# Forget logits in packets of 768 bytes, spread by GpSimd, and logit sums behind the scans

## The chip, the cores and the metric

One core of a Trainium2 chip runs the program. The metric is the device time of one execution in microseconds (us). TensorE (PE) does the matmuls and transposes, VectorE (DVE), ScalarE (ACT) and GpSimd (POOL) the element-wise work, and SyncE (SP) issues nearly all DMA transfers, in the order in which they are written.

## The reference

Gated linear attention over 4 batches, 8 heads, 768 tokens and 48 channels a head gives 3072 tokens of 384 channels. They pass a mixture of 8 experts with one expert a token, and then a block with two up-projections that are multiplied with each other and two projections behind them. The change touches the attention alone:

```python
f = 1.0 / (1.0 + np.exp(-f_logit))
for t in range(S):
    state = f[:, :, t, :, None] * state + np.einsum('bhd,bhe->bhde', k[:, :, t], v[:, :, t])
    y[:, :, t] = np.einsum('bhd,bhde->bhe', q[:, :, t], state)
...
logits = xn @ en.T / tau
expert_idx = np.argmax(logits, axis=1)
```

Here `f_logit` is stored as [batch, head, token, channel], so one token of one head is a run of 48 floats, 192 bytes, and neighbouring tokens of one head follow each other.

## The kernel before

The tokens are cut into 24 units of 128 (6 chunks of each of the 4 batches). The attention is a software pipeline that is written out by hand under `tc.manual_schedule()`: a loop of 26 turns (lines 758 to 788) calls a list of small steps, `parts` (lines 749 to 754), each on the unit that its second entry says: `(s_score, 2)` means that turn i works on unit i - 2. Every engine runs its instructions in the order in which the turns emit them, so the order in the list is the order in each queue.

For one unit, f is loaded to `fs` with the 128 tokens on the partitions and 8 heads of 64 columns (48 channels and a filling of ones). `s_pre` (line 398) makes the gate from the logits a turn ahead: ACT takes tanh(f/2), GpSimd scales it by 0.5 and adds 0.5, in place; only unit 0 does both on ACT, in two halves. `s_gate` (407) transposes the gates on PE, two heads at a time, four transposes into one PSUM bank, so that channels lie on the partitions and tokens along the row. `s_scan` (411) runs the two cumulative products on DVE. `s_qk` (427) transposes q and k and multiplies them by the products (`qd`, `kd`, on DVE); `s_score`, `s_mask`, `s_kb`, `s_inter`, `s_out`, `s_uu` do the attention inside the unit and the state. `s_xt` (518) transposes the result back and adds columns for the expert logits; ACT copies the tokens out, and `s_lg` (530) sums the logit columns on DVE, which releases the PSUM bank. Banks come from a pool of 6 in the order of use.

Beside this the pipeline converts weights that come as 64-bit numbers: `cvt.words` (248) on ACT reads a tile `raw`, `cvt.bits` (259) on DVE, `cvt.sums` (265) on GpSimd. The first `raw` tiles are needed in turn 6. `turn` is called four times a turn and takes the next piece of each routing generator `route` (565): ranking of the tokens on DVE and PE, then scatters of the tokens to DRAM, issued by GpSimd (624). `make_en` (538) normalises the expert vectors once, in pieces spread over turns 0 to 3.

At the end of each turn SP issues the loads: f of unit i + 3, k and q of i + 2, v of i (768 to 771), a `raw` tile, and in some turns a filling of the scatter target with zeros (786). `fs`, `ks`, `qs` have 3 buffers each. `load` (375) gives one DMA a unit and tensor: 128 partitions, 8 runs of 192 bytes on each. `warm` (385) issues matmuls on ones that compute nothing needed: 18 at the start, 24 in turn 0, 16 in turn 1.

Behind the attention come the routing's last groups, then the experts (`g1_step`, `g2_step`, with `xs_prep`, whose transposes at line 872 write every fourth word of a PSUM bank) and the last block (`ab_step`, `out_step`).

Of the kernel before, what the change touches and what calls it, by code (L numbers as in the profile page):

```python
# [7 lines left out]
F32 = mybir.dt.float32  # L8
# [3 lines left out]
AF = mybir.ActivationFunctionType  # L12
ALU = mybir.AluOpType
# [6 lines left out]
def attn_moe_glu_kernel(  # L20
# [18 lines left out]
    B, H, S, D = q.shape  # L39
    N, DM = out.shape  # L40
    E, _, FF = w1.shape
    P = 128
# [316 lines left out]
    ks = [ld.tile([P, H, 64], F32, name=f"k{i}") for i in range(NB)]  # L359
    fs = [ld.tile([P, H, 64], F32, name=f"f{i}") for i in range(NB)]  # L360
    NV = 4
# [13 lines left out]
    def load(src, tiles, u):  # L375
        if 0 <= u < NU:
# [4 lines left out]
            )  # L381

    st = {}

# [13 lines left out]
    def s_pre(u):  # L398
        for hs in (slice(H // 2, H), slice(0, H // 2)) if u == 0 else (slice(0, H),):
            f = fs[u % NB][:, hs, 0:D]  # L400
            A.activation(out=f, in_=f, func=AF.Tanh, scale=0.5)
            if u == 0:
                A.activation(out=f, in_=f, func=AF.Identity, scale=0.5, bias=half[:, 0:1])
            else:
                G.tensor_scalar(out=f, in0=f, scalar1=0.5, scalar2=0.5, op0=ALU.mult, op1=ALU.add)

    def s_gate(u):
        js = (range(NP // 2, NP), range(0, NP // 2)) if u == 0 else (range(NP),)
        st["f", u] = [(j[0], j[-1] + 1, tpair(fs[u % NB], "f", "acc", j)) for j in js]

# [127 lines left out]
    def make_en():  # L538
        spare = cv.tile([P, 512, 2], I32, name="raw", bufs=RAW)[0:E].bitcast(F32).rearrange("e n w -> e (n w)")
        raw, et = spare[:, 0:DM], spare[:, 512:512 + DM]  # L540
        ep = cv.tile([P, 512], F32, name="gt", bufs=2)[0:E].rearrange("e (h d) -> e h d", h=H)
        s = rt.tile([E, 6], F32, name="es")
        SP.dma_start(out=raw, in_=emb)
        SP.dma_start(out=s[:, 4:5], in_=tau.to_broadcast([E, 1]))
        yield
        G.memset(ep, 0.0)
        sq = wk.tile([P, DM], F32, name="sq", bufs=1)[0:E]
        A.activation(out=sq, in_=raw, func=AF.Square, accum_out=s[:, 0:1])
        G.tensor_tensor(out=s[:, 1:2], in0=s[:, 0:1], in1=half[0:E, 0:1], op=ALU.pow)
        G.tensor_scalar(out=s[:, 1:2], in0=s[:, 1:2], scalar1=1e-6, scalar2=None, op0=ALU.add)  # L550
        V.tensor_tensor(out=s[:, 2:3], in0=s[:, 1:2], in1=s[:, 4:5], op=ALU.mult)
        V.reciprocal(out=s[:, 3:4], in_=s[:, 2:3])
        yield
        G.tensor_tensor(out=et, in0=raw, in1=s[:, 3:4].to_broadcast([E, DM]), op=ALU.mult)
        G.tensor_tensor(out=ep[:, :, 0:D], in0=raw.rearrange("e (h d) -> e h d", h=H), in1=s[:, 3:4].unsqueeze(2).to_broadcast([E, H, D]), op=ALU.mult)
        yield
        b = bank([P, KD + NP, E], "eb")
        for j in range(KD):
            PE.transpose(out=b[:, j, :], in_=et[:, j * P:(j + 1) * P], identity=ident[0:E, 0:E])
        for j in range(NP):  # L560
            PE.transpose(out=b[:, KD + j, :], in_=ep[:, 2 * j:2 * j + 2, :].rearrange("e h d -> e (h d)"), identity=ident[0:E, 0:E])
        A.copy(out=enT, in_=b[:, 0:KD, :])
        A.copy(out=sel[:, :, 2 * D:], in_=b[:, KD:, :])

    def route(u0, n):
# [26 lines left out]
        V.tensor_reduce(out=nb, in_=O.rearrange("p g e -> p e g"), axis=AX.X, op=ALU.add)  # L592
        V.tensor_scalar(out=r0, in0=r0, scalar1=1e-6, scalar2=None, op0=ALU.add)
        yield
# [5 lines left out]
        for i in range(n - 1):  # L600
# [3 lines left out]
            )  # L604
        V.tensor_tensor(out=d, in0=L, in1=wide(mx), op=ALU.subtract)
        V.reciprocal(out=rinv, in_=r0)
        yield
# [70 lines left out]
    with tc.manual_schedule():  # L678
        for hs0 in (slice(H // 2, H), slice(0, H // 2)):
            SP.dma_start(out=fs[0][:, hs0, 0:D], in_=f_logit[0, hs0, 0:P, :].rearrange("h p d -> p h d"))  # L680
        load(k, ks, 0)
        load(f_logit, fs, 1)
        load(q, qs, 0)
# [3 lines left out]
        load(q, qs, 1)  # L687
        load(f_logit, fs, 2)
        V.memset(ones, 1.0)
        warm(18)  # L690
        V.memset(fs[0][:, :, D:], 1.0)
        G.memset(ident, 0.0)
# [9 lines left out]
        V.memset(half, 0.5)  # L702
        V.memset(half[:, 2:3], 0.0)
        for i in range(1, NB):
            V.memset(fs[i][:, :, D:], 1.0)
            V.memset(qs[i][:, :, D:], 0.0)
            V.memset(ks[i][:, :, D:], 0.0)
# [37 lines left out]
        def turn():  # L745
# [5 lines left out]
            (s_kb, 2), (cvt.lower, 2), (s_pre, -1), (cvt.sums, 1), (s_sm, 1), (s_xt, 4), (cvt.words, 0), (s_blocks, 2),  # L751
            (s_scan, 0), (turn, None), (turn, None), (turn, None), (turn, None), (cvt.bits, 0), (s_inter, 3), (s_lg, 4),
            (s_sq, 4), (s_out, 3), (cvt.upper, 1), (s_uu, 3),
# [4 lines left out]
        for i in range(NU + 2):  # L758
# [7 lines left out]
            if i - 4 in groups:  # L766
                routing.append(route(*groups[i - 4]))
            load(f_logit, fs, i + 3)
            load(k, ks, i + 2)
# [6 lines left out]
            if i in (0, 1):  # L776
                warm((24, 16)[i])
            if i == 0:
# [384 lines left out]
```

## Time and profile before

| | us |
|---|---|
| median of 3 runs | 741.42 (739.48 to 742.17) |
| profiled execution | 740.17 |
| its span, first to last instruction | 738.4 |
| attention stage in it, to the last score matmuls | about 151 |

The profile is of one execution. Times in it count from the span's start. An instruction's line number is that of the kernel before; a helper's line can be shared by several callers, and the tile names tell them apart. A row of a timeline gives start and duration in us, engine, line, operation, output<-inputs, shapes, the count of merged instructions and, in brackets, how long the engine stood idle before and what ended that. Matmuls overlap, so the duration of one is not its share of PE's time; the distance of two starts is.

### The profile page before, as it was taken

The page shows a single profiled execution, that of the slowest core. Times are in us where ns is not written, and L with a number is a line of the kernel's source. Part 1 is how long each engine was busy: PE and PEld are TensorE (multiplying, and loading weights), DVE is VectorE, ACT ScalarE, POOL GpSimd, SP SyncE. Part 2 cuts the span into 40 slices and gives each one's busy share as a digit, 9 for nine tenths or more (in the row PEclk, how much of TensorE's full clock was granted, in tenths as well). Part 3 has the DMA queues.
Part 4 walks back from the last instruction along what each step waited for, and adds up shares of the span by engine and source line. Part 5 has one row for each costly group of instructions (what it writes and reads, how often), then busy time and mean ns, then how long its engine had stood idle before and what let it go on. Part 6 is the DMA issues. An engine that isn't in the chain of part 4 may idle for free.

```text
span 738.4 us, 12730 instructions
## 1 busy us (share of the span) xinstructions
PE 721.0 (98%) x4849; PEld 663.9 (90%) x4849; DVE 347.2 (47%) x673; ACT 338.4 (46%) x703; POOL 338.9 (46%) x422
## 2 busy tenths in 40 slices
PE   7999999999999999999999999999999999999995
PEld 7989989988899998999999988988888888888885
DVE  7889899956564555354353232322322322323222
ACT  4688787864566575475554542112112122121210
POOL 6356696893977686474574862102202202221002
PEclk9999999999999999999999999999999999999999
DMA  8999999826668668745433330000100100100001
GB/s 170 219 199 212 224 242 213 217 94 203 213 198 263 211 209 255 222 145 153 129 124 93 123 87 1 15 29 1 44 1 0 44 1 0 44 1 19 25 1 46
DMA packets 132156, 86.47 MB, mean 117 GB/s; under 512 B 106481, under 2 KB 114681, under 8 KB 132089
## 3 DMA queue, kind: packets, MB, share of 16 engines
q1 hardware_dynamic: 128489, 75.34, 38.3%
q0 software_dynamic: 3072, 9.46, 3.4%
q8 instruction: 40, 0.66, 0.4%
q10 hardware_dynamic: 528, 0.79, 0.3%
q14 instruction: 27, 0.22, 0.1%
HBM read 70.57 MB, written 15.01 MB: 116 GB/s over the span
## 4 chain that ended last, share of the span: by engine, by line
PE 71%; issue 10%; POOL 6%; DMA 5%; DVE 3%; ACT 3%; SPq 1%; POOLq 0%; ACTq 0%; DVEq 0%
PE acc L899 13%; PE hb L885 12%; PE pa L981 10%; PE pb L981 10%; PE ob L994 10%; PE wpb L177 3%; PE a L442 2%; DMA stg<-in_moe_w_dram 2%; PE y L476 2%; POOL xsd L624 2%; PE xl L522 2%; DMA raw<-in_moe_w_out_dram 1%; PE y L468 1%; PE f L393 1%; PE xb L872 1%
## 5 line engine op out<-in xcount | busy, mean ns | idle before, releaser
L135 POOL TENSOR_TENSOR wl<-stg,wh 128x384 fp32r<-128x384 f32 (+1 forms) x121 | 138.6, 1175 | 61.9 <-ACT wh L134 60.0
L984 DVE TENSOR_TENSOR a<-a,pb 128x512 f32<-128x512 f32 x48 | 33.0, 687 | 181.6 <-PE pb L981 175.3
L994 PE MATMUL ob<-wp,ab 128*128 128x384 f32 x576 | 108.2, 339 | 0.0
L994 PEld LDWEIGHTS ob<-wp,ab 128*128 128x128 f32 x576 | 102.3, 188 | 3.8
L899 PE MATMUL acc<-h,wh 128*128 128x448 f32 (+7 forms) x384 | 104.2, 351 | 1.5 <-DVE h L888 1.0
L885 PE MATMUL hb<-xT,wh 128*128 128x448 f32 (+7 forms) x384 | 102.6, 348 | 0.0
L981 PE MATMUL pa<-x,wh 128*128 128x512 f32 x288 | 90.2, 394 | 0.0
L981 PE MATMUL pb<-x,wh 128*128 128x512 f32 x288 | 89.9, 393 | 0.0
L888 DVE SCALAR_TENSOR_TENSOR h<-hb,h 128x448 fp32r<-128x448 f32 (+7 forms) x64 | 37.0, 578 | 105.4 <-ACT h L887 104.9
L983 ACT COPY a<-pa 128x512 f32<-128x512 f32 x48 | 28.1, 586 | 120.6 <-PE pa L981 120.6
L1001 POOL DMA_INDIRECT out_dram<-o,didx x24 | 23.2, 965 | 129.4 <-DVE o L1000 126.0
L135 POOL TENSOR_TENSOR x<-xd,x 128x512 fp32r<-128x512 f32 x18 | 22.8, 1290 | 120.4 <-ACT x L134 120.4
L986 ACT CAST ab<-a 128x512 fp32r<-128x512 f32 x48 | 29.8, 621 | 104.5 <-DVE a L984 104.5
L134 ACT CAST wh<-stg 128x384 fp32r<-128x384 f32 (+1 forms) x124 | 62.7, 563 | 28.8 <-DMA stg<-in_moe_w_dram 22.4
L899 PEld LDWEIGHTS acc<-h,wh 128*128 128x128 f32 x384 | 70.4, 188 | 4.8 <-DVE h L888 2.2
L885 PEld LDWEIGHTS hb<-xT,wh 128*128 128x128 f32 x384 | 70.8, 188 | 1.4
L885 PE MATMUL hb<-xT,wl 128*128 128x448 f32 (+7 forms) x192 | 66.7, 348 | 0.0
L899 PE MATMUL acc<-h,wl 128*128 128x448 f32 (+7 forms) x192 | 66.7, 347 | 0.0
L981 PEld LDWEIGHTS pb<-x,wh 128*128 128x128 f32 x288 | 54.2, 188 | 12.7
L887 ACT ACTIVATE h<-hb 128x448 fp32r<-128x448 f32 (+7 forms) x64 | 32.4, 506 | 68.6 <-PE hb L885 68.4
L981 PEld LDWEIGHTS pa<-x,wh 128*128 128x128 f32 x288 | 53.6, 188 | 9.2
L981 PE MATMUL pb<-x,wl 128*128 128x512 f32 x144 | 56.9, 395 | 0.0
(185 smaller groups left out, 1288.5 us busy)
## 6 DMA issues: line engine op xcount, KB each, us to landing
stg<-in_moe_w_dram SPq DMA_DIRECT2D x31, 768.0 KB, 5.7
raw<-in_moe_w_dram SPq DMA_DIRECT2D x28, 512.0 KB, 5.3
xs<-xsd SPq DMA_DIRECT2D x8, 675.5 KB, 6.0
k<-in_k_dram SPq DMA_DIRECT2D x24, 192.0 KB, 5.2
q<-in_q_dram SPq DMA_DIRECT2D x24, 192.0 KB, 4.9
v<-in_v_dram SPq DMA_DIRECT2D x24, 192.0 KB, 4.5
f<-in_f_logit_dram SPq DMA_DIRECT2D x23, 192.0 KB, 3.9
raw<-in_moe_w_out_dram SPq DMA_DIRECT2D x8, 384.0 KB, 5.2
```

What stands on the lines that cost most here:

```text
L134: A.copy(out=hi, in_=src)
L135: eng.tensor_tensor(out=lo, in0=src, in1=f32(hi), op=ALU.subtract)
L885: PE.matmul(out=b, lhsT=w[x][:, kk, cs], rhs=xT[e][y][:, kk, :], start=(kk + n == 0), stop=(kk == KD - 1 and n == 2))
L887: A.activation(out=h[0], in_=b, func=AF.Relu)
L888: V.scalar_tensor_tensor(out=h[1], in0=b, scalar=0.0, in1=f32(h[0]), op0=ALU.max, op1=ALU.subtract)
L899: PE.matmul(out=acc[d], lhsT=w[x][:, s % 4, d * P:(d + 1) * P], rhs=hs[s][y], start=(s + n == 0), stop=(s == KF - 1 and n == 2))
L981: PE.matmul(out=b, lhsT=w[x][:, kk, cs], rhs=x2[n][y][:, kk, :], start=(kk + m == 0), stop=(kk == KD - 1 and m == 2))
L983: A.copy(out=t, in_=pa)
L984: V.tensor_tensor(out=t, in0=t, in1=pb, op=ALU.mult)
L986: A.copy(out=ab[s][0], in_=t)
L994: PE.matmul(out=oacc[t], lhsT=ab[s][x][:, t * P:(t + 1) * P], rhs=wp[:, y, s, :], start=(s + m == 0), stop=(s == KF - 1 and m == 2))
L1001: ins = G.indirect_dma_start(out=out, out_offset=bass.IndirectOffsetOnAxis(ap=didx[:, j:j + 1], axis=0), in_=o, in_offset=None,)
```

## The change

`load_f` takes the place of `load` for f of units 1 to 23. It issues four DMAs a unit, one for each pair of heads, each to 32 partitions: a partition holds four neighbouring tokens of two heads, so that a run is 4 x 48 floats, 768 bytes. ACT takes the tanh in this layout; GpSimd's scaling writes into a second tile, `gs`, of two buffers, where the heads are spread to 64 columns again; and `s_gate` transposes the four tokens of a partition one after the other and writes each to every fourth column of the bank. Unit 0 keeps its layout, in `gs[0]`. Beside that: `s_lg` moves from behind `s_inter` to directly behind `s_scan`, ahead of the routing pieces and `cvt.bits`; the add of 1e-6 to the norms in `route` moves from ahead of the rank matmuls to behind them; one product in `make_en` moves from DVE to GpSimd and the reciprocal behind it a turn later; and the warm-up matmuls of turn 0 go from 24 to 14.

```diff
-    fs = [ld.tile([P, H, 64], F32, name=f"f{i}") for i in range(NB)]
+    TQ = 4
+    fs = [ld.tile([P, 2, TQ * D], F32, name=f"f{i}") for i in range(NB)]
+    gs = [ld.tile([P, H, 64], F32, name=f"g{i}") for i in range(2)]
...
+    def load_f(u):
+        if 0 <= u < NU:
+            b, c = units[u]
+            for j in range(NP):
+                SP.dma_start(
+                    out=fs[u % NB][j * P // NP:(j + 1) * P // NP],
+                    in_=f_logit[b, 2 * j:2 * j + 2, c * P:(c + 1) * P, :].rearrange("h (p t) d -> p h (t d)", t=TQ),
+                )
...
     def s_pre(u):
-        for hs in (slice(H // 2, H), slice(0, H // 2)) if u == 0 else (slice(0, H),):
-            f = fs[u % NB][:, hs, 0:D]
+        if u:
+            f = fs[u % NB]
             A.activation(out=f, in_=f, func=AF.Tanh, scale=0.5)
-            if u == 0:
+            to = gs[u % 2].rearrange("p (t h) d -> p t h d", h=2)[:, :, :, 0:D]
+            G.tensor_scalar(out=to, in0=f.rearrange("p h (t d) -> p t h d", d=D), scalar1=0.5, scalar2=0.5, op0=ALU.mult, op1=ALU.add)
+        else:
+            for hs in (slice(H // 2, H), slice(0, H // 2)):
+                f = gs[0][:, hs, 0:D]
+                A.activation(out=f, in_=f, func=AF.Tanh, scale=0.5)
                 A.activation(out=f, in_=f, func=AF.Identity, scale=0.5, bias=half[:, 0:1])
-            else:
-                G.tensor_scalar(out=f, in0=f, scalar1=0.5, scalar2=0.5, op0=ALU.mult, op1=ALU.add)
 
     def s_gate(u):
-        js = (range(NP // 2, NP), range(0, NP // 2)) if u == 0 else (range(NP),)
-        st["f", u] = [(j[0], j[-1] + 1, tpair(fs[u % NB], "f", "acc", j)) for j in js]
+        if u == 0:
+            st["f", u] = [(j[0], j[-1] + 1, tpair(gs[0], "f", "acc", j)) for j in (range(NP // 2, NP), range(0, NP // 2))]
+            return
+        t = bank([P, NP, P], "f", "acc")
+        for i in range(TQ):
+            src = gs[u % 2][:, 2 * i:2 * i + 2, :].rearrange("p h d -> p (h d)")
+            PE.transpose(out=t.rearrange("q j (p t) -> q t j p", t=TQ)[:, i], in_=src, identity=ident)
+        st["f", u] = [(0, NP, t)]
...
-        V.tensor_tensor(out=s[:, 2:3], in0=s[:, 1:2], in1=s[:, 4:5], op=ALU.mult)
+        G.tensor_tensor(out=s[:, 2:3], in0=s[:, 1:2], in1=s[:, 4:5], op=ALU.mult)
+        yield
         V.reciprocal(out=s[:, 3:4], in_=s[:, 2:3])
-        yield
...
         V.tensor_reduce(out=nb, in_=O.rearrange("p g e -> p e g"), axis=AX.X, op=ALU.add)
-        V.tensor_scalar(out=r0, in0=r0, scalar1=1e-6, scalar2=None, op0=ALU.add)
         yield
...
         V.tensor_tensor(out=d, in0=L, in1=wide(mx), op=ALU.subtract)
+        V.tensor_scalar(out=r0, in0=r0, scalar1=1e-6, scalar2=None, op0=ALU.add)
         V.reciprocal(out=rinv, in_=r0)
...
-        load(f_logit, fs, 1)
+        load_f(1)
...
-        load(f_logit, fs, 2)
+        load_f(2)
...
-            (s_scan, 0), (turn, None), (turn, None), (turn, None), (turn, None), (cvt.bits, 0), (s_inter, 3), (s_lg, 4),
+            (s_scan, 0), (s_lg, 4), (turn, None), (turn, None), (turn, None), (turn, None), (cvt.bits, 0), (s_inter, 3),
...
-            load(f_logit, fs, i + 3)
+            load_f(i + 3)
...
-                warm((24, 16)[i])
+                warm((14, 16)[i])
```

## Rows read from the trace of the kernel before

**Rows 1.** The page: busy engines over the span; DMA share in 40 slices, in tenths.

```profile
PE 721.0 (98%) x4849; PEld 663.9 (90%) x4849; DVE 347.2 (47%) x673; ACT 338.4 (46%) x703; POOL 338.9 (46%) x422
...
DMA  8999999826668668745433330000100100100001
```

**Rows 2.** Stretches: length, busy us (instructions) of PE, PEld, DVE, ACT, POOL; clock, DMA share, GB/s.

```profile
8.00:19.00 11.00, 9.50 (x104) 8.67 (x104) 9.16 (x17) 4.50 (x11) 6.28 (x11) 1.00 1.00 197
34.00:37.00 3.00, 3.00 (x50) 2.85 (x50) 2.93 (x5) 1.35 (x3) 1.25 (x3) 1.00 1.02 346
190.00:200.00 10.00, 10.00 (x50) 9.16 (x49) 3.31 (x3) 4.79 (x11) 10.00 (x9) 1.00 0.99 336
```

**Rows 3.** Timeline of PE, line 442 alone: the score matmuls that open a turn.

```profile
15.48 1.16 PE L442 MATMUL a<-qd,kd 64*128 64x128 f32 x16 [1.45 <-DVE kd L434]
...
36.48 1.16 PE L442 MATMUL a<-qd,kd 64*128 64x128 f32 x16
43.96 1.16 PE L442 MATMUL a<-qd,kd 64*128 64x128 f32 x16
50.21 1.16 PE L442 MATMUL a<-qd,kd 64*128 64x128 f32 x16
...
62.71 1.16 PE L442 MATMUL a<-qd,kd 64*128 64x128 f32 x16
69.60 1.16 PE L442 MATMUL a<-qd,kd 64*128 64x128 f32 x16
...
107.76 1.16 PE L442 MATMUL a<-qd,kd 64*128 64x128 f32 x16
115.25 1.16 PE L442 MATMUL a<-qd,kd 64*128 64x128 f32 x16
```

**Rows 4.** Timelines of ACT and PE where they stood for a weight tile.

```profile
37.34 0.55 ACT L256 ACTIVATE gt<-raw 128x384 int32<-128x384 uint32 x1 [1.75 <-DMA raw<-in_moe_w_out_dram]
...
62.46 0.57 ACT L256 ACTIVATE gt<-raw 128x384 int32<-128x384 uint32 x1 [1.20 <-DMA raw<-in_moe_w_out_dram]
...
107.41 0.69 ACT L256 ACTIVATE g<-raw 128x512 int32<-128x512 uint32 x1 [1.45 <-DMA raw<-in_moe_w_dram]
...
39.69 0.63 PE L393 MATMUL kt<-ident,k 128*128 128x128 f32 x4 [1.03 <-ACT sq L528]
```

**Rows 5.** Timeline of the first 15 us: warm-up matmuls and DVE's first products.

```profile
5.44 2.77 PE L388 MATMUL warm<-ones 128*128 128x128 bf16 x24
...
9.63 0.69 DVE L433 TENSOR_TENSOR qd<-qt,w 128x512 f32<-128x512 f32 x1 [1.62 <-PE qt L393]
...
9.87 1.06 PE L388 MATMUL warm<-ones 128*128 128x128 bf16 x16
...
13.49 0.56 DVE L551 TENSOR_TENSOR es<-es 8x1 f32<-8x1 f32 x1
```

**Rows 6.** Line 378's issues on SP: ns min/median/max, first and last start.

```profile
L378 SPq DMA_DIRECT2D k<-in_k_dram x24: 395/1236/1922, 1.9 to 133.8; - x24
L378 SPq DMA_DIRECT2D q<-in_q_dram x24: 580/1796/4526, 3.0 to 135.0; - x24
...
L378 SPq DMA_DIRECT2D f<-in_f_logit_dram x23: 368/378/807, 2.4 to 128.1; - x23
```

**Rows 7.** The chain that ended last: start, us, what; transposes with and without strided output.

```profile
45.71 0.44 PE qt L393 x4
...
210.78 1.10 PE xb L872 x12
```

**Rows 8.** Line 405, GpSimd's scaling of the gates: ns min/median/max, first and last start.

```profile
L405 POOL TENSOR_SCALAR f<-f x23: 502/512/517, 6.5 to 137.8; 128x384 f32<-128x384 f32 x23
```

**Rows 9.** Timeline of DVE at 109 us: the logit sum and the bit operations before it.

```profile
109.60 0.68 DVE L262 TENSOR_SCALAR raw<-z 128x512 int32<-128x512 int32 x1
110.31 0.69 DVE L263 SCALAR_TENSOR_TENSOR raw<-z,raw 128x512 int32<-128x512 int32 x1
110.92 0.18 DVE L532 TENSOR_REDUCE lg<-xl 128x8 f32<-128x32 f32 x1
```

**Rows 10.** Timelines of ACT and GpSimd where the chain of scatters begins.

```profile
143.53 0.48 ACT L523 COPY xt<-xl 128x384 f32<-128x384 f32 x1 [1.27 <-PE xl L522]
...
147.53 1.22 POOL L449 TENSOR_SCALAR_AFFINE_SELECT am<-am 128x512 f32<-128x512 f32 x2 [2.02 <-ACT am L448]
```

More of the change, by code (lines that the diff above doesn't have):

```diff
@@ L679, in attn_moe_glu_kernel @@
         for hs0 in (slice(H // 2, H), slice(0, H // 2)):
-            SP.dma_start(out=fs[0][:, hs0, 0:D], in_=f_logit[0, hs0, 0:P, :].rearrange("h p d -> p h d"))
+            SP.dma_start(out=gs[0][:, hs0, 0:D], in_=f_logit[0, hs0, 0:P, :].rearrange("h p d -> p h d"))
         load(k, ks, 0)
-        load(f_logit, fs, 1)
+        load_f(1)
         load(q, qs, 0)
@@ L687, in attn_moe_glu_kernel @@
         load(q, qs, 1)
-        load(f_logit, fs, 2)
+        load_f(2)
         V.memset(ones, 1.0)
         warm(18)
-        V.memset(fs[0][:, :, D:], 1.0)
+        V.memset(gs[0][:, :, D:], 1.0)
         G.memset(ident, 0.0)
@@ L703, in attn_moe_glu_kernel @@
         V.memset(half[:, 2:3], 0.0)
+        V.memset(gs[1][:, :, D:], 1.0)
         for i in range(1, NB):
-            V.memset(fs[i][:, :, D:], 1.0)
             V.memset(qs[i][:, :, D:], 0.0)
```

## The prediction

> **What bounds the kernel now.** I read the page first. TensorE (PE) is busy 98% of the span and the DMA digits stand at 8 to 9 for the first eight slices, some 148 us, and fall after that [rows 1]. So the change, which touches only the attention stage at the head of the program, meets two nearly full resources there: PE and the 16 DMA engines. The table of stretches tells what fills the DMA engines: in 8 to 19 us, with nothing but the 192-byte packets of k, q, v and f on the way, a share of 1.00 moves 197 GB/s; in 34 to 37 us, with the 3072-byte rows of w_out, a share of 1.02 moves 346 GB/s; and in the bulk weight loads of 190 to 200 us, 0.99 moves 336 GB/s [rows 2].
>
> Next the timeline of PE at line 442, the score matmuls, which open every turn of the loop. Two neighbours tell the length of a turn: 43.96 to 50.21 is 6.25 us, and that is the time of the matmuls themselves: neither row shows idle time of PE before it. A longer turn holds a stall: 36.48 to 43.96 is 7.48, a stall of 1.2 us; 62.71 to 69.60 is 6.89, 0.6 us; 107.76 to 115.25 is 7.49, 1.2 us, of which I count 1.1 because that turn also holds the short routing matmuls. The turn before 15.48 shows a PE gap of 1.45 us that ended with DVE's kd [rows 3]. All that this change can take from the stage is in such stalls, about 5 us with the start; the rest of the stage is matmuls that it keeps. Then ACT and PE at those stalls: ACT stood 1.75, 1.20 and 1.45 us for a converted weight tile (raw) that had not landed, and PE's gap of 1.03 us in the first of them ended when ACT got through [rows 4]. So the stalls begin as late transfers and reach PE through ACT. Last the tail: at 143.53 ACT stood 1.27 us for PE, and at 147.53 GpSimd (POOL) stood 2.02 us for ACT [rows 10]. GpSimd's chain of scatters, which sets the end of the stage, therefore starts when PE gets there, and what PE gains before 143 us reaches the end one for one. Behind the stage the weights follow the routing result, so the same shift carries through.
>
> **The change part by part.** The sum is made against the profiled execution, 740.17 us (its span of 738.4 and 1.8 around it), which is 1.25 us below the median of 741.42.
>
> *The start.* The 24 warm-up matmuls of turn 0 last 2.77 us, 0.115 each [rows 5]; ten fewer free 1.1 us of PE ahead of the transposes that DVE's first qd waited 1.62 us for [rows 5]. Of this I take 0.95, because unit 0's q, issued behind three more f issues, may hold the last tenths. The es product at 13.49 takes DVE 0.56 us just before the next qd [rows 5]; it goes to GpSimd, and its reciprocal a turn later. Together 1.5 us at the score matmuls of 15.48, whose gap was 1.45 [rows 3]. It can't go below 0 by the rows as long as f of units 1 and 2 land no later.
>
> *The forget logits.* A load of 196,608 bytes at 197 GB/s takes 1.00 us of all DMA engines, and at the bulk rate of 336 GB/s 0.59 [rows 2]: the saving lies between 0 and 0.41 us a load. No row has 768-byte packets. At 197 GB/s one of 16 engines needs 15.6 ns for 192 bytes, at 346 and a share of 1.02 it needs 145 ns for 3072; a straight line between gives 41 ns for 768 bytes against 62 for four small ones. I take that, 0.33 us a load, as the two rows lie on both sides of the size.
>
> What that is worth hangs on the first raw tile, which ACT stood 1.75 us for at 37.34. If this tile lands no earlier, the 1.5 us of the start are lost there again. Ahead of it stand the f loads of units 1 to 7: seven times 0.33 is 2.3 us. Against that stand more issues: SP now issues four f transfers a unit, and one takes 0.378 us at the median [rows 6], 0.43 with the gap behind it. Nine more come before the loads of unit 2, 3.9 us of SP; a good part falls into time in which SP was held anyway (the median k and q issue takes 1.24 and 1.80 us, the shortest 0.40 and 0.58 [rows 6]). I put what shows at 1.1 us, an estimate. So the first raw tile lands 1.2 us earlier, and that, not the sum of start and stall, is the gain up to there. Bounds: 0 if nothing is saved, 2.7 (1.5 of the start and the stall of 1.2) if it lands early enough.
>
> Four units later ACT's wait of 1.20 us [rows 4] meets four more lighter loads, 1.3 us: the stall of 0.6 goes. Bounds 0 to 0.6.
>
> *Logit sums and routing.* In the turn from 107.76 PE's next transposes need the PSUM bank that the logit sum at 110.92 reads; that sum takes 0.18 us and stood behind the two bit operations of some 1.3 us [rows 9]. Directly behind the scans it no longer waits for these, nor for the routing pieces. DVE has the same work in the turn, so the delay moves to the next qd; that has room, as the score matmuls come some 4 us behind the bank. With the raw tile earlier as well (its wait was 1.45), I take 1.0 of the 1.1 here and 0.3 of a smaller stall (0.4) one turn before: 1.3, between 0.9 (the sum's move alone) and 1.5. The add of 1e-6 that moves behind the rank matmuls costs DVE the same 0.2 us, only no longer while GpSimd still computes the power; nothing is counted for it.
>
> *Edits at nothing.* The gate transposes now write every fourth word of PSUM. The transposes at line 872 do so already: twelve of 112 columns in 1.10 us, 92 ns each, and four q transposes of 128 packed columns take 0.44, 110 ns each [rows 7]; per column both are 0.82 to 0.86 ns, so 23 times 4 transposes cost nothing more. GpSimd's spread handles 384 elements as the old scaling did, 0.51 us [rows 8], in place of it, not beside it. Tanh has the same elements. A unit's f now frees its buffer when GpSimd has read it, a turn sooner than with the transposes; k and the rest behind it on SP profit or are indifferent. The 1.3 us of three more issues a unit hide behind SP's hold times of k and q; without that cover they are a rival below.
>
> Sum: 1.2 + 0.6 + 1.3 = 3.1 us off 740.17, 737.1; with the 1.25 to the median 738.3. With all lower bounds 0.9 us (740.5), with all upper ones 4.8 (736.6).
>
> [...]
>
> **The rivals.**
>
> *Everything goes.* All stalls vanish: 1.5 + 1.2 + 0.6 + 0.4 + 1.1 = 4.8, and some tenths in turns that I count as full: 5.3 us, 736.1. For it speaks that the f stream gets shorter in every unit and that stalls feed on each other; against it that the first raw tile comes too early in the program to collect seven full savings. 0.17.
>
> *The lighter packets don't relieve the DMA engines.* The four pieces take as much DMA time as the one did; then the first raw tile comes when it did, the start's gain is waited away there, 0.6 stays lost, and only the logit sum's move remains: 0.9 to 1.1, 740.4. For it speaks that the saving is interpolated; against it that 192-byte packets move 197 GB/s where long ones move 346 at the same share [rows 2]. 0.20. [...]
>
> *SP becomes the bound, slower.* If an issue among the pieces is held as k is, rather than passing at 0.38, three more cost 3 times 1.24, 3.7 us a unit. SP now spends 1.24 + 1.80 + 0.38 on k, q and f, 0.8 or so on v and as much on raw: 5.0 of a turn of 6.25. At 8.7 the loads fall behind by 2.5 us a turn; the decisive point is 6.25 us of issues a turn. With the longest f issue seen, 0.81 [rows 6], it is 5.0 + 2.9 = 7.9. The loads are a turn or more ahead, so some 15 turns would pay: from a few us at 6.5 up to 37, say 750. Against it: hold times of k and q are what a fuller queue makes, and that queue has less to move. 0.08.
>
> A smaller risk inside the forecast's range: the warm-up matmuls of 5.44 run at 115 ns, those of 9.87 at 66 [rows 5], and the granted clock reads 1.00 from 8 us on [rows 2]. If ten fewer delay that quicker pace, the start gives back up to 1.1 us.
>
> **How the numbers follow.** Forecast 0.55, everything goes 0.17, no relief 0.20, SP bound 0.08. A measurement of this kernel can tell about 0.5%, 3.7 us, from no change, that is 737.7. The forecast's own spread is 736.6 to 740.5 around 738.3; I put two fifths of it, 0.22, under 737.7. Faster: 0.22 + 0.17 and rounded up for the spread of the last case, 0.40; slower 0.08; same 0.52. For the range I take in the bounds and the two near rivals, and leave out SP as the bound: 735.3 to 741.3.
>
> **What would show it.** Right: f packets fall to a quarter in number; the 1.45 us gap before the second score matmuls shrinks; ACT's wait at the first raw tile stays near 1.5 us though it lands earlier; turns near 62 and 107 us last 6.25 to 6.4; the transposes of f last as before; the stretch from the last score matmuls to the first weight load keeps its length. Wrong: raw tiles land as late as before, SP's issues fill the turn, or the turns get longer than 6.25 in the matmuls themselves, which would mean that the strided writes cost after all.

## The result, and the profile after

The changed kernel takes 745.87 us at the median (742.52 to 750.62, 16 runs), the kernel before 740.93 beside it (739.48 to 743.36, 16 runs): a ratio of 1.0066, interval 1.0051 to 1.0081. It is slower, where 738.3 and a gain or no change were forecast. The profiled execution took 747.12 us, its span is 745.4.

The page of after: busy engines, the DMA share in 40 slices.

```profile
PE 723.3 (97%) x4839; PEld 666.8 (89%) x4839; DVE 347.4 (47%) x671; ACT 338.2 (45%) x703; POOL 339.8 (46%) x423
...
DMA  7888899914657676745333350010000100100001
```

Against [rows 1] the first digits are lower: the DMA engines, full before, now have pauses in the very stretch that the change was to relieve. The table of stretches of after shows it beside [rows 2]: in 8 to 19 us the share fell from 1.00 to 0.78 and the rate from 197 to 161 GB/s.

```profile
8.00:19.00 11.00, 10.40 (x108) 9.59 (x108) 9.17 (x17) 4.88 (x12) 4.71 (x10) 1.00 0.78 161
```

Where the time went is read from the score matmuls, now line 465, in the timeline of PE of after, with what lies between two of them:

```profile
36.17 1.16 PE L465 MATMUL a<-qd,kd 64*128 64x128 f32 x16
...
42.56 1.12 PE L481 MATMUL kb<-ident,kd 128*128 128x128 f32 x4 [3.77 <-ACT yT L504]
43.47 1.87 PE L545 MATMUL xl<-sel,yT 128*128 128x104 f32 x8
45.14 1.95 PE L491 MATMUL y<-qd,sbd 128*128 128x128 f32 x8
47.02 1.76 PE L499 MATMUL y<-am,v 128*64 128x128 f32 x16
...
49.17 1.16 PE L465 MATMUL a<-qd,kd 64*128 64x128 f32 x16
```

The turn that I call turn 6 (it ends with the seventh score matmuls) takes 13.00 us instead of 7.48 [rows 3]. The turns ahead of it are as long as before, so 5.5 of the 5.8 us by which the last score matmuls come later (157.15 for 151.31) lie in this one; the hand-over to the experts adds 2.1 (first expert matmul at 192.07 for 184.18). PE stands 3.77 us in it, where it stood 1.03 [rows 4], and then its own work takes longer: from kb to the next score matmuls 6.61 us, against 3.81 in the timeline of PE of before:

```profile
40.15 0.62 PE L458 MATMUL kb<-ident,kd 128*128 128x128 f32 x4
40.60 1.04 PE L522 MATMUL xl<-sel,yT 128*128 128x104 f32 x8
41.48 1.08 PE L468 MATMUL y<-qd,sbd 128*128 128x128 f32 x8
42.48 1.09 PE L476 MATMUL y<-am,v 128*64 128x128 f32 x16
```

The stretches of after tell why. From 40 to 42 us PE has nothing to do, and from 42 to 48 the granted clock reads 0.50, where it read 1.00 from 8 to 40 us here and from 34 to 50 us in the profile of before; these groups last nearly twice as long there (kb 1.12 us for 0.62, xl 1.87 for 1.04).

```profile
40.00:42.00 2.00, 0.00 (x0) 0.00 (x0) 1.16 (x3) 1.96 (x7) 0.00 (x0) 0.90 1.24 244
42.00:44.00 2.00, 1.44 (x7) 1.44 (x8) 2.00 (x4) 1.77 (x5) 0.87 (x2) 0.50 0.52 104
44.00:46.00 2.00, 2.00 (x11) 2.00 (x11) 1.93 (x5) 1.24 (x4) 1.59 (x3) 0.50 0.94 227
46.00:48.00 2.00, 2.00 (x16) 1.78 (x16) 1.28 (x5) 1.96 (x6) 0.73 (x2) 0.50 0.50 116
```

So the 5.5 us are 2.7 of longer standing and 2.8 of a lower clock. PE stood for ACT, and ACT for the first raw tile: 4.54 us instead of 1.75 [rows 4], although the start hardly moved (second score matmuls at 15.18 instead of 15.48).

```profile
39.83 0.54 ACT L256 ACTIVATE gt<-raw 128x384 int32<-128x384 uint32 x1 [4.54 <-DMA raw<-in_moe_w_out_dram]
```

The comparison rests on one profile of the kernel before, and that one was not its best. A second one is in the experiments (the kernel before with idle matmuls that come only behind the attention): there the first raw tile is issued at 29.13 us, ACT doesn't wait for it, turn 6 takes 6.35 us, and the last score matmuls come at 150.09.

```profile
37.01 1.16 PE L442 MATMUL a<-qd,kd 64*128 64x128 f32 x16
43.36 1.16 PE L442 MATMUL a<-qd,kd 64*128 64x128 f32 x16
```

Why the tile came late is seen on SP. The timeline of its issues, first before, then after (the zero fills of xsd mark the same two turns in both):

```profile
19.43 0.99 SPq L786 DMA_DIRECT2D xsd<-wp  x1
20.54 0.37 SPq L378 DMA_DIRECT2D f<-in_f_logit_dram  x1
21.00 1.45 SPq L378 DMA_DIRECT2D k<-in_k_dram  x1
22.50 0.86 SPq L378 DMA_DIRECT2D q<-in_q_dram  x1
...
24.41 2.57 SPq L786 DMA_DIRECT2D xsd<-wp  x1
...
30.80 1.78 SPq L246 DMA_DIRECT2D raw<-in_moe_w_out_dram  x3
```

```profile
22.24 0.88 SPq L809 DMA_DIRECT2D xsd<-wp  x1
23.21 3.09 SPq L392 DMA_DIRECT2D f<-in_f_logit_dram  x4
26.40 0.38 SPq L383 DMA_DIRECT2D k<-in_k_dram  x1
26.83 0.58 SPq L383 DMA_DIRECT2D q<-in_q_dram  x1
...
28.25 0.79 SPq L809 DMA_DIRECT2D xsd<-wp  x1
...
34.47 1.88 SPq L246 DMA_DIRECT2D raw<-in_moe_w_out_dram  x3
```

SP is 2.8 us late at the first fill, 3.8 at the second, 3.7 at the first raw tile. In the lines of line 383, its issues in after (ns min/median/max), k and q now pass at their shortest times, where [rows 6] has medians of 1236 and 1796 ns: what held them there is gone.

```profile
L383 SPq DMA_DIRECT2D k<-in_k_dram x24: 384/385/1393, 1.9 to 137.4; - x24
L383 SPq DMA_DIRECT2D q<-in_q_dram x24: 390/581/878, 4.4 to 138.5; - x24
```

But four f issues take 2.0 to 3.1 us. SP works without a pause (the gaps between the rows of its issues from 18.07 to 34.47 us are 0.10 us at most), and its issues set the pace of the loads; a turn's worth of them, 16.4 us for the three turns from 18.07 to the raw issue at 34.47, is 5.47 us where a turn of this stretch lasts 5.34.

### The profile page after: what moved, and what is told of

The parts are those of the page before. It is cut to its first block, busy times and chain, and to the rows that moved or that the text cites. A ratio compares the mean times of both kernels' runs of the same rounds, so it can differ in the third digit from the quotient of the medians.

```text
span 745.4 us, 12880 instructions
## 1 busy us (share of the span) xinstructions
PE 723.3 (97%) x4839; PEld 666.8 (89%) x4839; DVE 347.4 (47%) x671; ACT 338.2 (45%) x703; POOL 339.8 (46%) x423
## 4 chain that ended last, share of the span: by engine, by line
PE 75%; issue 9%; DMA 6%; POOL 3%; DVE 2%; ACT 2%; SPq 2%; POOLq 0%; DVEq 0%; ACTq 0%
PE acc L922 12%; PE hb L908 11%; PE pa L1004 10%; PE pb L1004 10%; PE ob L1017 10%; PE wpb L177 4%; PE y L499 3%; PE a L465 3%; PE xl L545 2%; DMA stg<-in_moe_w_dram 2%; PE y L491 2%; PE f L431 1%; PE qt L407 1%; DMA gd<-gt 1%; PE kt L407 1%
```

## The experiments

Theory A: SP's time for issues is what ran short; the first raw tile is late for that alone. Theory B: the packets are slow for the DMA engines (768 bytes, each transfer into 32 neighbouring partitions). Theory C: the small edits cost (the es product on GpSimd, the sums behind the scans, ten warm-ups fewer). What all runs gave, each beside the kernel before on its chip (medians of that 741.94 us in the first four rows of experiments, 737.45 in the next four, 738.3 to 738.4 in the rest); turn 6, the waits and the starts are from the one profiled execution of each kernel, which can differ from its median by some us:

| kernel | ratio to before (interval) | first raw issue, us | ACT's wait for it | turn 6 | last score matmuls | first expert matmul |
|---|---|---|---|---|---|---|
| before | 1 | 30.80 | 1.75 | 7.48 | 151.31 | 184.18 |
| changed | 1.0066 (1.0051 to 1.0081) | 34.47 | 4.54 | 13.00 | 157.15 | 192.07 |
| small edits alone | 0.9989 (0.9971 to 1.0007) | 29.75 | 0.91 | 6.64 | 148.83 | 184.39 |
| f loads alone | 1.0096 (1.0070 to 1.0121) | 35.05 | 4.30 | 12.43 | 156.04 | 191.86 |
| four issues of 192-byte packets | 1.0136 (1.0107 to 1.0165) | 36.28 | 4.48 | 12.93 | 158.56 | 194.21 |
| raw ahead of the turn's loads | 1.0095 (1.0062 to 1.0128) | 28.95 | 0.00 | 10.51 | 154.44 | 189.83 |
| every fourth partition | 1.0230 (1.0203 to 1.0257) | 40.17 | 4.14 | 14.60 | 164.53 | 202.50 |
| idle matmuls in turn 6 | 1.0068 (1.0049 to 1.0086) | 33.86 | 3.99 | 9.70 | 153.85 | 186.80 |
| two issues of 384-byte packets | 1.0062 (1.0041 to 1.0082) | 31.09 | 1.03 | 6.75 | 151.21 | 188.03 |
| packets from unit 7 on | 1.0052 (1.0025 to 1.0080) | 30.47 | 0.00 | 6.25 | 150.10 | 183.13 |
| changed, again | 1.0104 (1.0070 to 1.0138) | 35.02 | 3.77 | 12.25 | 156.45 | 189.24 |
| idle matmuls in turn 6, again | 1.0092 (1.0067 to 1.0117) | 34.35 | 3.94 | 9.66 | 155.99 | 188.80 |
| two of four issues by ScalarE | 1.0064 (1.0040 to 1.0089) | 30.15 | 0.00 | 6.25 | 150.27 | 186.85 |
| 384 bytes, one of two by ScalarE | 1.0059 (1.0032 to 1.0085) | 28.34 | 0.00 | 6.25 | 148.60 | 186.65 |

**One part alone.** The small edits on the old loads, and the new loads without the small edits (24 warm-ups, the sums where they were).

> The kernel before with all the small edits (logit sums behind the scans, the add of 1e-6 moved, the product on GpSimd, 14 warm-up matmuls) and its old f loads. If the new f loads cause the loss (theory A: four issues a unit hold up SP, so the first weight tile comes late and PE first stands and then runs at the lower clock; theory B: the packets themselves are served slowly), this lies at 738.5 to 741 and the turn after 36 us lasts 7.5 us as before. If the small edits cause it (theory C: above all the ten warm-up matmuls), it lies near 745 with a longer turn or a lower clock somewhere.

> The kernel before with the new f loads, the spreading and the new gate transposes alone; 24 warm-up matmuls and the old order of the logit sums. A and B: near 746, with ACT's wait at the first weight tile of 4 us or more, a turn of about 13 us there and a granted clock of about 0.66 in 40 to 50 us. C: 740 to 742.

The loads alone make the loss, turn 6 and all. The small edits bring the last score matmuls 2.5 us forward (1.3 against the second profile of the kernel before) and nothing at the end: theory C falls, and so does a step of the prediction (below).

**Issues without packets.** The kernel before, with the f load cut into four issues of the old packets.

```diff
+    def load_f(u):
+        if 0 <= u < NU:
+            b, c = units[u]
+            for j in range(NP):
+                SP.dma_start(
+                    out=fs[u % NB][:, 2 * j:2 * j + 2, 0:D],
+                    in_=f_logit[b, 2 * j:2 * j + 2, c * P:(c + 1) * P, :].rearrange("h p d -> p h d"),
+                )
...
-            load(f_logit, fs, i + 3)
+            load_f(i + 3)
```

> The kernel before, each f load cut into four issues of two heads on all 128 partitions, packets of 192 bytes as before, same layout. It has the issues without the packets. A: slower than before by about as much as the change or more (743 to 748), since it saves no DMA time: first weight tile late, PE standing over 3 us, lower clock behind it. B: as before (740 to 742), the number of issues being no matter.

No long packet, no GpSimd spread, and the same late tile (PE stood 4.84 us for it), with a DMA share of 0.75 from 8 to 19 us. The number of issues is enough to do it.

**The order.** The raw loads moved ahead of the turn's f, k, q and v.

> The changed kernel with the weight tiles issued ahead of the turn's f, k, q and v instead of behind them; nothing else. A: the first tile is issued some 5 us earlier, ACT's wait of 4.5 us goes, PE doesn't stand there and the clock stays at 1.00: 736 to 740, below both kernels. B: the tiles gain a place but the queue is as slow; the wait shrinks by half and the total stays above 741. C: near 745 still.

A miss for my numbers: ACT's wait for the raw tile is gone, but now the tanh waits for its f, in the timeline of ACT of this kernel, and PE for GpSimd's scaling behind the tanh; the last line is the stretch:

```profile
38.13 0.52 ACT L415 ACTIVATE f<-f 128x384 f32<-128x384 f32 x1 [4.21 <-DMA f<-in_f_logit_dram]
...
39.37 1.03 PE L431 MATMUL f<-ident,g 128*128 128x128 f32 x4 [2.52 <-POOL g L417]
...
40.00:42.00 2.00, 2.00 (x11) 2.00 (x10) 1.94 (x4) 1.96 (x7) 0.00 (x0) 0.50 0.79 161
```

Not one tile but the whole stream is behind; the order only says who waits.

**Other partitions.** `out=fs[u % NB][j:P:NP]` in place of `[j * P // NP:(j + 1) * P // NP]`, with the gate transposes' output to match.

> The four forget-logit issues of a unit keep their 768-byte packets, but each writes every fourth partition instead of 32 neighbouring ones (the output pattern of the gate transposes changes to match). Theory A (SP's issues come too late): nothing changes, 746 to 747 us, turn 6 about 13 us, DMA share between 8 and 19 us about 0.78. Theory B (packets into 32 neighbouring partitions get in one another's way): the DMA engines finish sooner, the raw wait before turn 6 shrinks from 4.5 us to about 2, and the time falls to 741 to 743 us.

Neither theory foresaw 755 us. The lines of SP, this kernel first, then the changed one (ns min/median/max), fit theory A:

```profile
L392 SPq DMA_DIRECT2D f<-in_f_logit_dram x92: 598/604/1482, 2.4 to 142.7; - x92
```

```profile
L392 SPq DMA_DIRECT2D f<-in_f_logit_dram x92: 312/426/1742, 2.4 to 133.6; - x92
```

An issue with strided partitions holds SP 0.60 us instead of 0.43, and everything behind it slides further; the first raw tile goes out at 40.17. For B it says nothing either way, as SP hides what the DMA engines would do.

**Fewer issues.** Four heads and two tokens a partition: two issues a unit of 384-byte packets. And the changed kernel with the old single load for units 1 to 6.

> The changed kernel with two issues a unit of 384-byte packets (four heads, two tokens a partition) instead of four of 768. Theory A goes by issues: SP is spared two of the three extra issues, some 0.8 us a unit, so by turn 6 about five units, 4 us; the raw wait falls to about 1.5 to 2.5 us, the clock holds in turn 6, turn 6 takes 7 to 9 us, the time 740 to 742 us. If it were the size of the packets (each slower than the four small ones it stands for), the time would lie halfway, 743 to 744 us.

> The changed kernel, but the forget logits of units 1 to 6 come as before, by one issue of 192-byte packets each; packets of 768 bytes from unit 7 on (loads issued from turn 4). Theory A (issues of the first turns, when the DMA engines were never without work, put the queue behind): turn 6 falls back to 7 to 8.5 us and the time to 740 to 742 us, though 52 of the 92 packet loads remain. If the packet loads cost something in every turn, the loss shrinks by less than half, 743 us and above.

Both take turn 6 back, to 6.75 and 6.25 us, so its loss is made by the issues for units 1 to 6, which go out ahead of turn 4. Those of the later units, as many a turn (68 of the 92; the 52 of the expectation is a slip), cost little in sum: from the seventh score matmuls to the last it takes 107.6 us, in the two profiles of the kernel before 107.4 and 106.7. With two issues a unit SP is still late now and then: ACT stood 3.30 us for a raw tile at 56.87, and that turn took 8.11 us. The times are another matter: 1.0062 and 1.0052, so neither is back at the kernel before, as I had expected of both.

**Another issuer.** `(A if j > 1 else SP).dma_start(...)` in the changed kernel, and `(A if j else SP)` in the one with two issues.

> The changed kernel, but two of a unit's four packet loads are issued by ScalarE instead of SyncE. Theory A (SP's time for issues is what is short): the queue of SP is relieved of two issues a unit, the DMA share between 8 and 19 us rises from 0.78 to 0.9 or more, the first raw tile is issued by 32 us, turn 6 takes 6.3 to 8 us, and the time is 3 to 6 us below the changed kernel beside it, less what ScalarE's own issues cost (two a unit, bounded by nothing and by 0.8 us in each of 20 turns). If the DMA engines or the packets were what is slow, moving the issues changes nothing: turn 6 stays at 12 to 13 us.

> Packets of 384 bytes in two issues a unit, one of them by ScalarE: SP has as many issues as in the kernel before. Theory A: no raw wait before turn 6, turn 6 at 6.25 us, the last score matmuls 1 to 3 us earlier than in the kernel before, and the time at 0.995 to 1.0 of it. If packets in 64 partitions cost the DMA engines something of their own, the raw waits of turns 6, 9 and 10 stay at 1 us and more and the time at 1.003 or above.

In the first the same packets go into the same partitions, and turn 6 is 6.25 us: B is not needed. ScalarE brings its own queue along with its time, though (q10 moves 4208 packets in the first, 528 in the changed kernel), and no run tells the two apart: that SP's own time is short, and that its one queue takes no more, are both theory A here. The times miss what I expected: beside the changed kernel's 745.01 us the two take 742.39 and 742.96, so of its 6.6 us above the kernel before some 2 to 3 came back, not all (see the hand-over below). The stretches from 8 to 19 us, two of four by ScalarE first, then 384 bytes with one by ScalarE:

```profile
8.00:19.00 11.00, 9.87 (x94) 9.01 (x92) 9.17 (x18) 4.39 (x10) 3.87 (x9) 1.00 0.86 183
```

```profile
8.00:19.00 11.00, 10.01 (x112) 9.18 (x113) 9.47 (x18) 5.51 (x12) 4.89 (x10) 1.00 1.04 217
```

The second moves 217 GB/s at a full share, against 197 before [rows 2]: with the longer packets the DMA engines moved a little more at a full share, once the issues kept up. It is not one run's luck: the three profiles with these loads have 214 to 217 GB/s in this stretch, the six with the old loads 196 to 205.

**What the clock costs.** 56 idle matmuls of 128 columns ahead of the key transposes, in the gap of turn 6; and the changed kernel and this one once more, side by side.

```diff
-        kt = tpair(ks[u % NB], "kt")
+        kt = bank([P, NP, P], "kt")
+        if u == 6:
+            for _ in range(56):
+                PE.matmul(out=kt[:, 0, :], lhsT=ones, rhs=ones)
...
```

> The changed kernel with 56 idle matmuls of 128 columns put ahead of the key transposes of the unit that stands in turn 6 (into the bank that these transposes overwrite). If the lower granted clock is a cost of its own behind the late transfer, the clock from 42 to 48 us stays near its upper level, the groups there take 0.9 us instead of 1.7, turn 6 falls from 13.0 to about 10 to 10.5 us, and the time to about 743 us. If the late transfer alone makes the loss, turn 6 stays at 12.5 to 13.5 us and the time at 746 to 747 us; the extra matmuls may add up to 3 us if they stand on the path.

> The changed kernel as it is, on the chip of the three runs beside it, so that they can be set against it: 1.005 to 1.008 of the kernel before, turn 6 about 13 us.

> The kernel with 56 idle matmuls in turn 6, once more beside the changed kernel: in its first profile turn 6 took 9.70 us, 3.3 less. If that carries to the end, it is 2.5 to 3.5 us faster than the changed kernel beside it; if the hand-over to the experts takes it back, within 1 us of it.

They last 3.29 us, the clock stays at 1.00, and turn 6 shrinks by 3.3 and 2.6 us: the clock of 0.50 is about half of what is lost there. At the end no gain is seen: 745.15 against 745.01 us side by side, though five runs each, spread over 3 and 6 us, would not show one of 2 us. In the first profile the 3.3 us lasted to the last score matmuls (153.85 for 157.15); in the second later turns gave back 2.1 of the 2.6 us, with waits for raw tiles of 3.14 and 2.63 us: the loads were still behind, and a turn that comes earlier meets them earlier.

**Why an earlier end of attention was not an earlier end.** Four kernels of the table end the score matmuls 1.0 to 2.7 us before the profile of the kernel before does, and none is faster. (Against its second profile, 150.09, only the small edits alone and 384 bytes with ScalarE are ahead. And one of the four did carry its gain over: packets from unit 7 on, first expert matmul at 183.13, in the quickest of its five runs, 735.64 us.) In the one with 384 bytes and ScalarE, the timeline of PE where attention hands over to the experts (xb are the transposes of the first expert's tokens), and the stretch:

```profile
179.23 0.31 PE L895 MATMUL xb<-ident,xs 112*128 112x112 f32 x1 [3.00 <-ACT xs L886]
180.67 2.31 PE L895 MATMUL xb<-ident,xs 112*128 112x112 f32 x11 [1.13 <-DVE xs L884]
182.66 4.19 PE L177 MATMUL wpb<-wo,w3t 128*128 128x384 f32 x12
...
182.00:186.00 4.00, 4.00 (x16) 4.00 (x15) 1.87 (x3) 1.12 (x3) 0.00 (x0) 0.50 0.50 186
```

Against the same groups in the timeline of before:

```profile
180.56 1.69 PE L872 MATMUL xb<-ident,xs 112*128 112x112 f32 x12 [0.81 <-ACT xs L863]
182.02 2.33 PE L177 MATMUL wpb<-wo,w3t 128*128 128x384 f32 x12
```

PE had used up its work on w3 and stood for the tokens; then the granted clock read 0.50 from 182 to 186 us, and the 12 products ahead of the experts took 4.19 us for 2.33. To tell the clock from the loads, idle matmuls went there too: 24 ahead of the last w3 transposes, 48 ahead of the first xb (`warm(24)`, `warm(48)`), and in the last two kernels fewer (24; 24 and 24), in a bank of the other pool.

> The kernel before with idle matmuls at two places of the hand-over from attention to the experts: 24 ahead of the last transposes of w3 and 48 ahead of the first token transposes. In its profile the engine stood there for 0.73 and 0.81 us and kept its clock, so they can only cost: 0 to 3 us slower (72 x 0.059 = 4.2 us of work, less 1.5 us of gaps), nothing gained.

> The small edits alone (loads as before) with the same idle matmuls. Theory H (an attention stage that ends 2.5 us earlier loses it in the hand-over, because TensorE runs out of work there and falls to the lower clock): no stretch below 0.95 between 165 and 190 us, and the time 1 to 3 us below the kernel before (0.996 to 0.999). If the loads of tokens and weights set the end of the hand-over whatever the clock, the time stays at 0.998 to 1.002.

> Two issues a unit of 384 bytes, one of them by ScalarE, with the same idle matmuls. Without them its attention ended 2.7 us earlier than in the kernel before, TensorE then stood 3.0 and 1.1 us ahead of the token transposes, the granted clock fell to 0.50 and the product behind took 3.9 us instead of 2.1. Theory H: the clock stays, 2.5 to 3 us come back, 0.998 to 1.003. If not the clock but the loads decide: 1.005 to 1.008 as without.

> The changed kernel with the same idle matmuls. Its profile shows no lower clock in the hand-over (the granted clock was 1.00 from 170 to 200 us), so theory H gives nothing here in such runs, and takes back some of its slower ones: 1.005 to 1.009, turn 6 at 12 to 13 us as without.

> The small edits alone, with only the 24 idle matmuls ahead of the last transposes of w3, in a bank of the other pool so that they need not wait for VectorE as they did in the run before (where they started after 1.37 us of standing and lengthened TensorE's work by 1.5 us, and the 48 behind them by 2.7 us). Theory H: the engine doesn't stand, the clock stays at 1.00 from 165 to 190 us, the first product of the experts starts at 181.5 to 182.5 us instead of 184.2, and the time is 0.995 to 0.998 of the kernel before: a version that beats both. If the token load decides (8.1 us in one run of it, 6.5 in others), 0.998 to 1.001.

> Two issues a unit of 384 bytes, one by ScalarE, with 24 idle matmuls at each of the two places, in a bank of the other pool. Theory H: the clock stays, the idle matmuls stand in the gaps, 1 us or so better than with 72: 0.998 to 1.002. If the token load decides, as with 72: 1.001 to 1.004.

| kernel with idle matmuls | ratio to before (interval) | last score matmuls | first expert matmul |
|---|---|---|---|
| before, 72 | 1.0046 (1.0027 to 1.0065) | 150.09 | 185.30 |
| small edits, 72 | 1.0034 (1.0017 to 1.0051) | 148.68 | 184.48 |
| 384 bytes and ScalarE, 72 | 1.0024 (1.0006 to 1.0042) | 149.26 | 184.45 |
| changed, 72 | 1.0096 (1.0075 to 1.0118) | 155.99 | 191.14 |
| small edits, 24 | 1.0024 (1.0007 to 1.0041) | 148.49 | 185.00 |
| 384 bytes and ScalarE, 24 and 24 | 1.0041 (1.0025 to 1.0058) | 149.27 | 186.44 |

With 72, the 384-byte kernel fell from 742.96 to 739.84 us beside equal runs of before (738.42 and 738.38), the clock read 1.00 from 165 to 195 us, and the same products took 2.34 us: about the 3 us of the clock came back (the two were measured on different chips). What is left, 1.5 us, is open. The controls say the same from the other side: before, where the clock reads 1.00 from 165 to 190 us without it, the idle work only cost (3 us), and the changed kernel stayed where it was. With the small edits the 48 stood in the way, 2.86 us on a PE that had work, while the 24 ran behind a wait that PE had anyway:

```profile
170.00 1.50 PE L388 MATMUL warm<-ones 128*128 128x128 bf16 x24 [1.37 <-DVE w3t L169]
...
176.39 2.86 PE L388 MATMUL warm<-ones 128*128 128x128 bf16 x48
```

With the 24 alone PE stood ahead of xb, 0.72 us for ACT and, one matmul later, 1.15 for DVE (180.04), and the clock fell again, to 0.66 on the mean of 180 to 185 us. That was a miss for my 0.995 to 0.998:

```profile
180.04 2.12 PE L872 MATMUL xb<-ident,xs 112*128 112x112 f32 x11 [1.15 <-DVE xs L861]
...
180.00:185.00 5.00, 4.96 (x23) 4.83 (x24) 2.19 (x4) 1.60 (x3) 0.00 (x0) 0.66 0.70 223
```

The last row missed its 0.998 to 1.002 as well: there the first 24 themselves stood 2.43 us for DVE, and the clock read 0.71 from 170 to 175 us.

Which load decided is seen on ACT. The first expert weights were asked for at 172.04 us in the kernel before and used at 176.46; with the small edits and 24 they were asked for 2.8 us earlier, at 169.26, and used at 175.97, 6.7 us later instead of 4.4. ACT scales the tokens (xs) behind them. The timelines of ACT, before and this one:

```profile
176.46 1.14 ACT L134 CAST wh<-stg 128x512 fp32r<-128x512 f32 x2 [2.56 <-DMA stg<-in_moe_w_dram]
...
179.89 1.12 ACT L863 ACTIVATE xs<-xs 112x384 f32<-112x384 f32 x2 [1.40 <-DMA xs<-xsd]
```

```profile
175.97 1.14 ACT L134 CAST wh<-stg 128x512 fp32r<-128x512 f32 x2 [3.68 <-DMA stg<-in_moe_w_dram]
...
177.91 1.12 ACT L863 ACTIVATE xs<-xs 112x384 f32<-112x384 f32 x2
```

In the kernel before ACT stood once more for the tokens; in this one they had landed, and their scaling came straight behind the casts that had stood for the weights. So here the weights decided, not the tokens. From request to use they took 4.4 and 4.8 us in the two profiles of the kernel before, 4.7, 4.6 and 5.6 in the three of the changed one, but 6.9 with two of four by ScalarE, 7.2 and 7.0 with 384 bytes and ScalarE (in a third profile ACT didn't stand for them), 7.1 with two issues from SP alone. With the small edits they took 4.6 and 4.7, and only in this profile 6.7. So it goes partly by the kernel and partly by the run; why is open. No kernel tried beats the one before: the small edits alone, 0.9989, come nearest and can't be told from it.

## Why the prediction was wrong, step by step

*What bounds the kernel: right, with a hole.* The stalls did begin as late transfers and reached PE through ACT, at the turn named. But "the DMA engines are full" was read as what limits the loads. They were kept full through SP, which had some time to spare; the change took that time away, and then the engines stood (a share of 0.78 for the 1.00 of [rows 2]).

*The failed step: nine more issues put at 1.1 us, and three a unit said to hide behind SP's hold times.* The mechanism was half right: the hold times of k and q did go (1.24 to 0.39 and 1.80 to 0.58 us at the median), 2.1 us a unit. But against them stood an f of 0.37 that became 2.0 to 3.1 us; four at the median of 0.43 would be 1.7, but single ones took up to 1.3 us in that stretch, and what held those is open. And in the list of SP's work per turn, 5.0 of 6.25 us, two things were mis-sized. The zero fills of xsd, 0.8 to 0.9 us unheld, were not in it; and the turn that SP has to keep up with is 5.34 us in the first turns, not 6.25. With these, f 2.6, k 0.4, q 0.6, v 0.9 and a fill of 0.8 are 5.3: no slack. The lag measured 2.1 us when f of unit 4 went out (13.25 for 11.12), where 1.1 was put, and 3.7 at the first raw issue, so 1.5 more came in the turns where nothing was put. Of the 3.7, 2.5 remained at the landing (the wait ended at 39.83 instead of 37.34), where the prediction had the tile 1.2 us earlier.

*The stalls of one execution taken for the kernel's.* The 1.2 and 0.6 us that were to be won at raw tiles come from a single profile. In the second profile of the kernel before both are absent: turn 6 takes 6.35 us, the turn at 62 us 6.27, and ACT waits for no raw tile in them. That part of the gain was not there to be had in every run.

*The price of a late tile.* It was taken as the length of the wait. PE stood 3.77 us and then ran at a granted clock of 0.50 (42 to 48 us), which doubled the price: 2.8 us of the 5.5.

*The rival "SP becomes the bound"* (0.08, some 750 us) was the case, in its sign and at over half its size (4.9 us for some 8.6), by another road. It was to need issues held as k was and to bill some 15 turns of 6.25 us at 2.5 each. In fact lightly held ones were enough (0.6 us each on the mean of the three turns), the lag came at the start and in the turns of 5.34, and it was paid in one turn. "The packets don't relieve" was not the case, though its number would have been nearer: with SP relieved, 384-byte packets moved 217 GB/s for 197. What 768 bytes give with SP free was not seen at a full share (0.86). Four pieces of 48 KB in place of one of 192 KB, with the old packets, cost 1.4% (1.0136); what the runs show of the reason is the issuing queue.

*The start: 1.5 us, of which the changed kernel shows 0.3* at the second score matmuls (0.6 and 0.7 in its other two profiles), the small edits alone 1.1 (14.34 us). Whether the small risk named at the end of the rivals came true can't be told. The first four q transposes did take longer in the changed kernel (1.06 us for 0.73), but they took 1.06 in the second profile of the kernel before too, with its 24 warm-ups, and 0.63 with the small edits alone, with 14: the pace there goes by the run.

*The stall of 0.6 near 62 us* is gone in the profile (61.67 to 67.92 is 6.25) and in the second a turn of 7.62 stands there, so nothing follows from it. *The logit sums, 1.3 us:* the two turns from 101 to 115 took 14.16 before, 13.85 with the small edits alone, 14.32 in the changed kernel. The later of the two gained 0.8 with the small edits and the earlier lost 0.5: 0.3 remains, the term was four times too large.

*Edits at nothing: right.* The gate transposes with their strided output and GpSimd's spread, in the changed kernel:

```profile
L431 PE MATMUL f<-ident,g x16: 272/273/329, 21.3 to 37.6; 128*128 128x128 f32 x16
...
L417 POOL TENSOR_SCALAR g<-f x4: 502/512/513, 20.7 to 35.1; 128x384 f32<-128x384 f32 x4
```

0.512 us is what the old scaling took [rows 8], and four transposes take 0.59 us in the chain of after as in that of before.

*"What PE gains before 143 us reaches the end one for one": wrong.* It rested on one row where GpSimd waited [rows 10]. The small edits alone brought 2.5 us to the last score matmuls and 0 to the first expert matmul. Behind the scatters stand three things that end close to each other: PE's work on w3, the token load and the first weights; where a load was last, PE stood there, and the clock fell in some profiles (0.50 behind stands of 3.00 and 1.13 us with 384 bytes and ScalarE) and not in others (1.00 behind the 0.81 us of before). A loss went through (5.8 us became 7.9, in the second profile of the changed kernel 5.1 stayed 5.1); of a gain mostly little was left (of 2.5 us nothing, with packets from unit 7 on 1.1 of 1.2).

## What to carry to other kernels

Before splitting a transfer, add up the issues of its queue per turn, with everything else that the queue issues, and set the sum against the shortest turn, not the mean one. A sum of durations that nothing held up is only a lower bound: here it would be 4.4 us (f four times its median of 0.43), where 5.3 were measured. Don't take full DMA engines for a queue with time to spare: here a share of 1.00 fell to 0.78 with three more issues a unit. With longer packets keep the issue count of the queue (fewer, longer issues, or a second engine that issues): from 8 to 19 us 384 bytes, one of two issues by ScalarE, moved 217 GB/s, four issues of 768 bytes from SP alone 161, the old loads 197. Read a stall in more than one profile before you count on winning it back. Price a wait of TensorE with what the clock does after it (here 2.8 us behind a stand of 3.77), and don't carry a gain past a hand-over where several things end together.

## What the runs showed of the hardware that was not expected

- An issue of f held SP 0.43 us at the median for 32 neighbouring partitions and 0.60 for every fourth one, at the same bytes and packets.
- A stand of PE of 3.77 us (turn 6) was followed by a granted clock of 0.50, and so were one of 2.52 (raw ahead of the turn's loads) and two of 3.0 and 1.13 with one matmul between (the hand-over); 56 idle matmuls of 59 ns in the gap of turn 6 kept it at 1.00.
- DMA engines that look saturated (share 1.00) fell to 0.78, and to 0.75 with the old packets, when one queue got three more issues a unit.
- At a full DMA share from 8 to 19 us, packets of 192 bytes alone moved 196 to 205 GB/s, those with f in packets of 384 bytes 214 to 217.
